# An instruction planner's queue order: X's coordinate rows ahead of Y, a longer plan time for transposing loads, one guard product by a scalar, and the last rows in two stores

## The chip, the cores and the metric

The kernel runs on one core of one Trainium2 chip. The metric is the device time of one execution in microseconds. All inputs and outputs are in HBM; the result is the 2048 x 512 output in bfloat16.

## What is computed

A gated mix of two branches over the same x (2048 x 512): attention with 32 query heads of size 16 that share one key and one value head, and a gMLP with a spatial product over the 2048 rows.

```python
def reference(A_x, A_wq, A_wk, A_wv, A_wo, B_x, B_w_in, B_w_sp, B_b_sp, B_w_out, gate_w):
    x = A_x
    g = _sigmoid((x * gate_w).sum(-1, keepdims=True))
    a = _A_ref(x, A_wq, A_wk, A_wv, A_wo)      # softmax(q k^T / 4) v, 32 heads of 16, one k and one v
    b = _B_ref(x, B_w_in, B_w_sp, B_b_sp, B_w_out)
    return g * a + (1 - g) * b
...
    z = _gelu(jnp.einsum('bsd,df->bsf', x, w_in))
    z1, z2 = z[..., :Fh], _layernorm(z[..., Fh:], axis=-1)      # Fh = 688
    g = jnp.einsum('ts,bsf->btf', w_sp, z2) + b_sp[None, :, None]
    return jnp.einsum('bsf,fd->bsd', z1 * g, w_out)
```

## The kernel before

The kernel does not form the 2048 x 2048 attention weights. It replaces the exponential by a polynomial of third degree, sums the keys and values into moments once, and evaluates for each query a form of degree three in its 16 coordinates. A guard measures the largest query and key norms, and a second, general path (L1128, "slow") runs instead if they are too large; here the first path runs.

Work on the queries is cut into 16 units u = 4 tg + G: tg is a group of 512 rows, G a group of eight heads. For one unit:

- `g_q` (L813) computes the queries Qt on TensorE, ScalarE copies them, and SyncE (SP) writes them to a scratch in HBM, `qe` (L824, four writes).
- `y_load` (L831) reads them back: Y (L833), in two halves of 512 KB, spreads each coordinate over the partitions; X's coordinate rows (L836, two small reads, tag "lin") fill rows 56 to 63 and 120 to 127 of X. X's other rows are squares that ScalarE makes (L850, after TensorE's L846). Both X and Y have two buffers, so unit u takes those of unit u - 2.
- Four times, t and h being 0 or 1, TensorE multiplies X by the moments T3 (L877, four matmuls, "W"); the result fills PSUM banks 0 to 3, always the same ones. VectorE reads the first half of it and multiplies by Y (L888, "Pr"); ScalarE copies the other half to Wt (L892) and GpSimd multiplies it by Y (L893). TensorE then sums over the coordinates (Pr,cs) and adds terms that read X directly (X,M and X,T3d) and Qt (Qt,T2b).
- After the four units of a group, `g_den` (L906) forms the denominators (Rh) and OT (L927), `g_out` (L1011) adds the output products.

In between TensorE does the gMLP: wT (the transposed spatial weights, loaded by transposing DMAs, L975, four for each of four row groups) times z, in groups of 16 steps ahead of which a bias row stands (bspz,ones), evacuated by VectorE (L995, L998), and the output products with wout and wo.

The order is not written by hand. Every operation is added to a list with a priority, a planned duration and what it reads and writes; `Plan.run` (L348) then simulates the five engines with these durations and always takes, of what is ready on the engine that is free first, the lowest priority number. That gives each engine's instruction order; on the chip, engines wait for each other with semaphores. So a number in the plan can move rows on all engines. For DMAs the plan has the time that SP is held and a rate; Y of unit u has priority YPRI + u and YPRI + u + 0.1, the qe writes YPRI + u - 0.1.

The last four output tiles (t2 = 12 to 15) are stored at the very end; SP branches on the guard's flag ahead of the first of them.

Of the kernel before, what the change touches and what calls it, by code (L numbers as in the profile page):

```python
# [10 lines left out]
ALU = mybir.AluOpType  # L11
# [33 lines left out]
DMA_RATE = 230.0  # L45
# [4 lines left out]
YPRI = 2.1  # L50
# [247 lines left out]
class Plan:  # L298
# [8 lines left out]
    def add(self, eng, cost, fn, r=(), w=(), pri=50.0, grp=None, evac=False, dma=0, size=0, chan=None, rate=DMA_RATE, tag="", after=(), opens=(), hold=(), slack=0.0, swp=SWITCH_PRI):  # L307
        t = Task()
        t.alt = eng if isinstance(eng, dict) else {eng: (cost, fn)}
        t.dma, t.bytes, t.chan, t.rate = dma, size, chan, rate  # L310
        t.pri, t.grp, t.tag, t.idx = pri, grp, tag, len(self.tasks)
        t.first = False
        t.users, t.op, t.eng = [], None, None
        t.tiles = getattr(fn, "tiles", WHOLE)
        r, w = list(r), list(w)
        if grp is not None:
            k = ("grp", id(grp))
            if evac:
# [12 lines left out]
        t.opens = [self.lastw[k] for k in opens]
        t.gates = list(hold)
        t.slack = slack
        t.swp = swp
        for d in t.deps:
            d.users.append(t)
        for d in t.opens + t.gates:
            d.users.append(t)
        t.left = len(t.deps) + len(t.opens) + len(t.gates)
        for k in r:  # L340
            self.readers.setdefault(k, []).append(t)
        for k in w:
# [149 lines left out]
def build_kernel(nc, x_d, wq_d, wk_d, wv_d, wo_d, win_d, wsp_d, bsp_d, wout_d, gw_d, out_d):  # L492
    es = ExitStack()
    with es:
        block = es.enter_context(nc.Block())

        def sb(name, shape, dt):
            return es.enter_context(nc.sbuf_tensor(name, shape, dt))

        def dap(t, off, ap):  # L500
            return bass.AP(tensor=t.tensor, offset=off, ap=ap)
# [3 lines left out]
        def bank(b, n=512, off=0):  # L505
            return ps[:, 512 * b + off:512 * b + off + n]
# [7 lines left out]
        qe = nc.dram_tensor("qe", (16 * 16, QP), B16).ap()  # L514
# [33 lines left out]
        X = sb("X", [128, NXU, 4, 512], B16)  # L548
# [6 lines left out]
        outsb = sb("outsb", [128, 4, D], B16)  # L555
# [14 lines left out]
        qk1 = sb("qk1", [128, 8], F32)  # L570
# [25 lines left out]
        out2 = out_d.rearrange("b s d -> (b s) d")  # L596
# [3 lines left out]
        add = pl.add  # L600
# [31 lines left out]
        def load(eng, fn, w, r=(), size=0, n=1, pri=0.0, chan=None, rate=DMA_RATE, tag="", after=(), hold=()):  # L632
            if chan is None:
                chan = "d%d" % nd[0]
                nd[0] += 1
            return add(eng, 3000.0 if rate < DMA_RATE else 560.0 * n, fn, r=r, w=w, dma=16 * n, size=size, pri=pri, chan=chan, rate=rate, tag=tag, after=after, hold=hold)

        def nonc(fn):
            def f(q):
# [11 lines left out]
        def ld_x(c):  # L651
            load("sp", lambda q: q.dma_start(xn[:, 4 * c:4 * c + 4, :], x2[512 * c:512 * c + 512, :].rearrange("(k p) n -> p k n", p=128)), [("xn", c)], size=524288, pri=c, tag="x")
        ld_x(0)
        load("sp", lambda q: q.dma_start(ident[:], id_d), ["id"], size=32768, pri=0)
        for h in range(2):
            load("sp", lambda q, h=h: q.dma_start(win[:, :, FH + 344 * h:FH + 344 * h + 344], win_d[:, FH + 344 * h:FH + 344 * h + 344].rearrange("(dt p) n -> p dt n", p=128)), [("win2", h)], size=352256, pri=0)
# [172 lines left out]
        def y_load(u):  # L829
            o0 = 16 * QP * u  # L830
            yb, ub = u % NY, u % NXU  # L831
            for h in range(2):
                yld[0] = load("sp", lambda q, h=h: q.dma_start(Y[:, yb, 2 * h:2 * h + 2, :, :].rearrange("p j e n -> p (j e n)"), dap(qe, o0 + 2048 * h, [[QP, 16], [0, 8], [1, 2048]])), [("Y", yb, h)], r=[("qe", u)],  # L833
                              size=524288, pri=YPRI + u + 0.1 * h, chan="y%d%d" % (yb, h), tag="Y")

            load("sp", lambda q: [q.dma_start(X[64 * e + 56:64 * e + 64, ub, :, :], dap(qe, o0 + 512 * e, [[QP, 8], [1024, 4], [1, 512]])) for e in range(2)],  # L836
                 [("X", ub, j) for j in range(4)], r=[("qe", u)], size=65536, n=2, pri=YPRI + u + 0.3, chan="lin%d" % ub, tag="lin")

        def squares(u):
            s, ub = u % NQT, u % NXU  # L840
# [18 lines left out]
        def unit(u):  # L859
# [140 lines left out]
        def zl(t2, ft):  # L1000
            if ft < 5:
                return z1[:, ft, 128 * t2:128 * t2 + 128]
            o = 256 * (t2 // 4) + 128 * (t2 % 2)
            return z5[:, o:o + 128]

        def wl(t2, ft):
            return wout[:, ft + (t2 % 4) // 2 if ft == 5 else ft, :]

        tail = []

        def g_out(t2):  # L1011
            tg, i = t2 // 4, t2 % 4
            last = tg == 3
            g = Group("L" if last else "F")
            opens = [] if last else [("z1", ft, tg) for ft in range(6)] + [("OT", tg % 2, 3)]
            for G in range(4):
                add("pe", c_mm(512), mmx(lambda: g.b, 512, 0, OT[:, tg % 2, G, 128 * i:128 * i + 128], wo[:, G, :], G == 0, False), r=["wo", ("OT", tg % 2, G)], grp=g, pri=25, tag="out", opens=opens if G == 0 else [])
            for ft in range(6):
                add("pe", c_mm(512), mmx(lambda: g.b, 512, 0, zl(t2, ft), wl(t2, ft), False, ft == 5), r=["wout", "wout5", "wout6", ("z1", ft, tg)], grp=g, pri=25, tag="out")
            k = t2 % 4  # L1020
            ea = (620.0, lambda a: a.activation(outsb[:, k, :], bank(g.b), ACT.Copy, scale=G1[:, t2:t2 + 1]))  # L1021
            ed = (640.0, lambda v: v.tensor_scalar(outsb[:, k, :], bank(g.b), G1[:, t2:t2 + 1], None, ALU.mult))  # L1022
            add({"act": ea, "dve": ed} if last else {"act": ea}, 0, None, r=["G1"], w=[("ob", k)], grp=g, evac=True, pri=3, tag="fin")
            o = load("sp", lambda q: q.dma_start(out2[128 * t2:128 * t2 + 128, :], outsb[:, k, :]), [("out", t2)], r=[("ob", k)], size=131072, pri=0, chan="o%d" % k, tag="out")
            if last:
                tail.append(o)

# [36 lines left out]
        for tg in range(4):  # L1066
            for G in range(4):
                u = 4 * tg + G
# [29 lines left out]
            return [t.matmul(ps[0:32, 512 * gf.b + 128 * i:512 * gf.b + 128 * i + 128], qkb[:, i, :], ident[:], start=True, stop=True, tile_position=(0, 0)) for i in range(2)]  # L1098
        add("pe", 120.0, fl, r=["qkb", "id"], grp=gf, pri=12, tag="flag")
        add("dve", 350.0, lambda v: v.tensor_reduce(qk1[0:32, 0:2], ps[0:32, 512 * gf.b:512 * gf.b + 256].rearrange("p (i n) -> p i n", i=2), AX.X, ALU.max), w=["qk1"], grp=gf, evac=True, pri=30, tag="guard")  # L1100
        add("dve", 80.0, lambda v: v.tensor_tensor(qk1[0:32, 2:3], qk1[0:32, 0:1], qk1[0:32, 1:2], ALU.mult), r=["qk1"], w=["qk2"], pri=30, tag="guard")  # L1101
        add("dve", 80.0, lambda v: v.tensor_scalar(qk1[0:32, 3:5], qk1[0:32, 0:2], QK_MAX, None, ALU.is_le), r=["qk1"], w=["qk3"], pri=30, tag="guard")
        add("dve", 80.0, lambda v: v.tensor_scalar(qk1[0:32, 5:6], qk1[0:32, 2:3], S_MAX * S_MAX / SLACK, None, ALU.is_le), r=["qk2"], w=["qk4"], pri=30, tag="guard")
        add("dve", 80.0, lambda v: v.tensor_reduce(qk1[0:32, 6:7], qk1[0:32, 3:6], AX.X, ALU.min), r=["qk3", "qk4"], w=["qk5"], pri=30, tag="guard")
# [209 lines left out]
def bass_gated_mix__grouped_kv_mqa__mixer_gmlp__prompt_kernel(  # L1314
    nc, A_x, A_wq, A_wk, A_wv, A_wo, B_x, B_w_in, B_w_sp, B_b_sp, B_w_out, gate_w, out,
):
    build_kernel(nc, A_x, A_wq, A_wk, A_wv, A_wo, B_w_in, B_w_sp, B_b_sp, B_w_out, gate_w, out)
# [29 lines left out]
```

## Time and profile before

| | |
|---|---|
| runs | median 281.47 us, 281.13 to 281.86, three runs |
| profiled execution | 281.9 us, its span 280.1 us |
| granted TensorE clock, mean | 0.997 |
| instructions in the span | 10009 |
| busy shares of TensorE, VectorE, ScalarE, GpSimd | 94%, 62%, 61%, 57% |
| chain that ended last | TensorE 78%, DMA 8%, VectorE 5%, ScalarE 4% |

Times inside the span are counted from its start. In a row of the timeline stand start, duration, engine, line, operation, output and inputs, shapes and how many; in square brackets how long the engine was idle before and what released it. In a row by stretch stand the stretch, its length and each engine's busy time in it (TensorE, its weight loads, VectorE, ScalarE, GpSimd), the granted clock, the share of the DMA engines and GB/s.

### The profile page before, as it was taken

What the parts mean: (1) busy time and instruction counts of PE and PEld (TensorE: products, weight loads), DVE (VectorE), ACT (ScalarE), POOL (GpSimd) and SP (SyncE); (2) the same over time, 40 slices, a digit from 0 to 9 for tenths busy, and PEclk for the clock granted to TensorE, in tenths of its full rate; (3) what the DMA queues carried; (4) which work ended last, traced back from release to release, by engine and by line L of the source; (5) the groups of instructions that cost most, each with busy time, mean ns of one, the idle gap of its engine ahead of it and who ended that gap; (6) DMA issues with size and microseconds to landing.
All of it is one profiled execution on the core that took longest, in us unless ns stands there. A gap on an engine that the chain in (4) does not pass through costs nothing.

```text
span 280.1 us, 10009 instructions
## 1 busy us (share of the span) xinstructions
PE 263.9 (94%) x4356; PEld 121.0 (43%) x4359; DVE 173.3 (62%) x318; ACT 170.8 (61%) x231; POOL 159.2 (57%) x93
## 2 busy tenths in 40 slices
PE   8899999998799999999898999899997999999991
PEld 3587654532243433533343434333442534344560
DVE  2697995474557966554679657635967463695202
ACT  3576888899695656676764856477545468542001
POOL 8693130474938585665857584757657475986000
PEclk9999999999999999999999999999999999999998
DMA  7949937016777988479882615498986335300002
GB/s 195 331 152 273 218 83 148 6 38 169 241 181 101 234 134 197 99 188 224 163 197 61 173 30 159 107 179 125 235 95 164 82 100 154 68 4 4 2 2 80
DMA packets 51019, 37.80 MB, mean 135 GB/s; under 512 B 36021, under 2 KB 46618, under 8 KB 50970
## 3 DMA queue, kind: packets, MB, share of 16 engines
q1 hardware_dynamic: 50970, 37.12, 57.3%
q8 instruction: 35, 0.57, 0.9%
q14 instruction: 14, 0.11, 0.1%
HBM read 24.52 MB, written 4.19 MB: 103 GB/s over the span
## 4 chain that ended last, share of the span: by engine, by line
PE 78%; DMA 8%; DVE 5%; ACT 4%; SPq 2%; issue 1%; DVEq 0%; ACTq 0%
PE ps L608 51%; PE ps L603 12%; PE ps L877 10%; DMA X<-qe 6%; PE ps L956 3%; DVE Pr L888 2%; DMA wT<-in_A_x_dram 2%; PE ps L846 2%; ACT Wt L892 1%; ACT X L850 1%; ACT Q L826 1%; ACT Qt L820 1%; DVE qk L1101 1%; ACT Ns L901 0%; DVE outsb L1022 0%
## 5 line engine op out<-in xcount | busy, mean ns | idle before, releaser
L893 POOL TENSOR_TENSOR Pr<-Wt,Y 128x1024 bf16<-128x1024 bf16 x64 | 136.3, 2130 | 80.1 <-ACT Wt L892 50.0
L888 DVE SCALAR_TENSOR_TENSOR Pr<-ps,T1c,Y 128x1024 bf16<-128x1024 f32 x64 | 82.0, 1282 | 49.4 <-PE ps L877 49.0
L892 ACT ACTIVATE Wt<-ps,T1c 128x1024 bf16<-128x1024 f32 x64 | 71.4, 1116 | 55.7 <-PE ps L877 55.3
L608 PE MATMUL ps<-wT,z 128*32 128x512 bf16 x1280 | 84.8, 380 | 0.0
L608 PEld LDWEIGHTS ps<-wT,z 128*32 128x32 bf16 x1280 | 32.4, 97 | 35.7 <-issue 8.6
L877 PE MATMUL ps<-X,T 64*128 64x512 bf16 x256 | 38.8, 381 | 4.3 <-DVE Pr L888 4.1
L850 ACT ACTIVATE X<-ps 128x1024 bf16<-128x1024 f32 x32 | 31.3, 1022 | 9.8 <-PE ps L846 9.7
L608 PE MATMUL ps<-wout,z 128*32 128x512 bf16 x384 | 26.8, 380 | 0.5 <-DVE z L998 0.5
L995 DVE TENSOR_TENSOR z<-ps,z 128x512 bf16<-128x512 f32 x20 | 13.7, 687 | 13.8 <-PE ps L608 13.6
L603 PE MATMUL ps<-win,xT 128*128 128x344 bf16 x128 | 21.3, 309 | 0.1
L877 PEld LDWEIGHTS ps<-X,T 64*128 64x128 bf16 x256 | 7.3, 94 | 30.0 <-DVE Pr L888 15.7
L608 PE MATMUL ps<-Pr,cs 128*32 128x512 bf16 x256 | 20.0, 381 | 0.0
L937 ACT ACTIVATE z<-ps 128x344 bf16<-128x344 f32 x32 | 14.1, 460 | 7.9 <-PE ps L603 6.2
L608 PE MATMUL ps<-wo,win 128*32 128x512 bf16 x256 | 18.0, 380 | 0.0
L1021 ACT ACTIVATE outsb<-ps,G 128x512 bf16<-128x512 f32 x14 | 9.5, 689 | 13.6 <-PE ps L608 13.6
L902 DVE SCALAR_TENSOR_TENSOR Prd<-ps,T1d,Qt 128x512 bf16<-128x512 f32 x16 | 11.9, 747 | 7.1 <-PE ps L608 6.9
L608 PEld LDWEIGHTS ps<-wout,z 128*32 128x32 bf16 x384 | 9.8, 96 | 11.8 <-issue 2.6
L608 PE MATMUL ps<-xT,wq 128*32 128x512 bf16 x224 | 14.5, 380 | 0.3 <-DVE qm L1049 0.2
L927 DVE SCALAR_TENSOR_TENSOR win<-Ns,S,ps 128x512 bf16<-128x512 f32 x16 | 11.7, 741 | 5.0 <-PE ps L608 5.0
L939 DVE BATCH_NORM_STATS2 bst<-z 128x6 f32<-128x344 bf16 x32 | 14.3, 486 | 0.7 <-ACT z L937 0.7
L967 ACT ACTIVATE z<-ps 128x512 bf16<-128x512 f32 x20 | 11.8, 599 | 4.5 <-PE ps L608 2.6
L603 PEld LDWEIGHTS ps<-win,xT 128*128 128x128 bf16 x128 | 11.5, 97 | 6.0 <-ACT z L937 0.8
(138 smaller groups left out, 285.4 us busy)
## 6 DMA issues: line engine op xcount, KB each, us to landing
Y<-qe SPq DMA_DIRECT2D x32, 512.0 KB, 5.0
wT<-in_A_x_dram SPq DMA_DIRECT2D x4, 512.0 KB, 6.0
qe<-Qt SPq DMA_DIRECT2D x64, 32.0 KB
out_dram<-outsb SPq DMA_DIRECT2D x16, 128.0 KB, 2.8
X<-qe SPq DMA_DIRECT2D x32, 32.0 KB
Pr<-c_third SPq DMA_DIRECT2D x1, 784.0 KB, 9.1
win<-in_B_w_in_dram SPq DMA_DIRECT2D x2, 344.0 KB, 4.7
win<-in_B_w_in_dram SPq DMA_DIRECT2D x1, 688.0 KB, 9.5
```

The source lines that it names most:

```text
L603: return lambda t: t.matmul(bank(b(), n, off), lhsT, rhs, start=start, stop=stop)
L608: return [t.matmul(ps[32 * q:32 * q + 32, 512 * b() + off:512 * b() + off + n], lhsTs[q], rhss[q], start=start, stop=stop, tile_position=( ...
L850: add("act", 1030.0, lambda a, h=h: a.activation(X[:, ub, 2 * h:2 * h + 2, :], bank(g.b + 2 * h, 1024).rearrange("p (j n) -> p j n", j=2), ...
L877: return [p.matmul(bank(gw.b + 2 * i + e), T3[64 * e:64 * e + 64, t, :], X[64 * e:64 * e + 64, ub, 2 * h + i, :], start=True, stop=True, t ...
L888: add("dve", 1290.0, lambda v, wv=wv, pi=pi, yv=yv, t=t: v.scalar_tensor_tensor(Pr[:, pi, :, :], wv(), T1c[:, t:t + 1], yv, ALU.add, ALU.m ...
L892: add("act", 1040.0, lambda a, wv=wv, wi=wi, t=t: a.activation(Wt[:, wi, :, :], wv(), ACT.Identity, bias=T1c[:, t:t + 1]), r=["T1c"], w=[( ...
L893: add("pool", 2130.0, lambda v, wi=wi, pi=pi, yv=yv: v.tensor_tensor(Pr[:, pi, :, :], Wt[:, wi, :, :], yv, ALU.mult), r=[("Y", yb, h), ("W ...
L902: add("dve", 750.0, lambda v: v.scalar_tensor_tensor(Prd[:, u % NPD, :], bank(gd.b), T1d[:, 0:1], Qt[:, s, :], ALU.add, ALU.mult), r=["T1d ...
L937: add("act", 456.0, lambda a, g=g, h=h: a.activation(z2[:, FH * st + 344 * h:FH * st + 344 * h + 344], bank(g.b, 344), ACT.Gelu_apprx_tanh ...
L939: add("dve", 495.0, lambda v, h=h: v.bn_stats(bst[:, st, h, :], z2[:, FH * st + 344 * h:FH * st + 344 * h + 344]), r=[("z2", st, h)], w=[( ...
L967: add("act", 540.0, lambda a: a.activation(z1[:, ft, 512 * tc:512 * tc + 512], bank(g.b), ACT.Gelu_apprx_tanh), w=[("z1", ft, tc)], grp=g, ...
L995: add("dve", 690.0, lambda v: v.tensor_tensor(dst, bank(g.b), dst, ALU.mult), w=[("z1", ft, tc)], grp=g, evac=True, pri=3.5, tag="u")
```

## The change

Four edits, in the functions above. Transposing loads hold SP 4000 instead of 3000 ns in the plan. X's coordinate rows get a priority just under that of their unit's Y instead of behind it. One product of the guard, 32 x 1 elements, is written as tensor by per-partition scalar instead of tensor by tensor. The last four output tiles go out in two stores of two tiles instead of four.

```diff
-            return add(eng, 3000.0 if rate < DMA_RATE else 560.0 * n, fn, ...
+            return add(eng, 4000.0 if rate < DMA_RATE else 560.0 * n, fn, ...
...
             load("sp", lambda q: [q.dma_start(X[64 * e + 56:64 * e + 64, ub, :, :], ...
-                 ... size=65536, n=2, pri=YPRI + u + 0.3, chan="lin%d" % ub, tag="lin")
+                 ... size=65536, n=2, pri=YPRI + u - 0.05, chan="lin%d" % ub, tag="lin")
...
-            o = load("sp", lambda q: q.dma_start(out2[128 * t2:128 * t2 + 128, :], outsb[:, k, :]), ...
-            if last:
-                tail.append(o)
+            if not last:
+                load("sp", lambda q: q.dma_start(out2[128 * t2:128 * t2 + 128, :], outsb[:, k, :]), ...
+            elif k % 2:
+                tail.append(load("sp", lambda q: q.dma_start(out2[128 * t2 - 128:128 * t2 + 128, :].rearrange("(k p) n -> p k n", p=128), outsb[:, k - 1:k + 1, :]), ...
+                                 r=[("ob", k - 1), ("ob", k)], size=262144, pri=0, ...
...
-        add("dve", 80.0, lambda v: v.tensor_tensor(qk1[0:32, 2:3], qk1[0:32, 0:1], qk1[0:32, 1:2], ALU.mult), ...
+        add("dve", 80.0, lambda v: v.tensor_scalar(qk1[0:32, 2:3], qk1[0:32, 0:1], qk1[0:32, 1:2], None, ALU.mult), ...
```

Lines behind the edits move by one or two in the changed kernel (L1101 of the guard becomes L1103, L1024 becomes L1025 or L1027). The orders of the two programs are alike up to the first product of unit 3; from there they differ on all engines. Three places follow.

TensorE, unit 3, from its second product (L877) to its fourth, before:

```order
L877 MATMUL ps<-X,T 128x512 x4
L608 MATMUL ps<-X,M 32x512 x4
L608 MATMUL ps<-Rh,sg 32x128 x16
L608 MATMUL ps<-wT,z 32x512 x8
L608 MATMUL ps<-Qt,T2b 32x512 x4
L608 MATMUL ps<-wT,z 32x512 x20
L877 MATMUL ps<-X,T 128x512 x4
L608 MATMUL ps<-wT,z 32x512 x4
L608 MATMUL ps<-bspz,ones 32x512 x4
L608 MATMUL ps<-wT,z 32x512 x24
L877 MATMUL ps<-X,T 128x512 x4
```

and after:

```order
L877 MATMUL ps<-X,T 128x512 x4
L608 MATMUL ps<-X,M 32x512 x4
L608 MATMUL ps<-Rh,sg 32x128 x16
L608 MATMUL ps<-wT,z 32x512 x24
L877 MATMUL ps<-X,T 128x512 x4
L608 MATMUL ps<-wT,z 32x512 x4
L608 MATMUL ps<-Rh,sg 32x128 x16
L608 MATMUL ps<-wT,z 32x512 x4
L877 MATMUL ps<-X,T 128x512 x4
```

Between the last two products there now stand eight 512-column matmuls and sixteen of 128 columns instead of 32 of 512 columns.

TensorE, unit 6, from its third product to what follows the fourth, before:

```order
L877 MATMUL ps<-X,T 128x512 x4
L608 MATMUL ps<-Q,cs 32x128 x4
L608 MATMUL ps<-wT,z 32x512 x4
L877 MATMUL ps<-X,T 128x512 x4
L608 MATMUL ps<-bspz,ones 32x512 x4
L608 MATMUL ps<-X,T3d 32x512 x4
```

and after:

```order
L877 MATMUL ps<-X,T 128x512 x4
L608 MATMUL ps<-wout,z 32x512 x8
L608 MATMUL ps<-wT,z 32x512 x8
L608 MATMUL ps<-X,T3d 32x512 x4
L877 MATMUL ps<-X,T 128x512 x4
L608 MATMUL ps<-bspz,ones 32x512 x4
```

Two short rows (a norm's sum, Q,cs, and one step of wT) have become 20 matmuls of 512 columns.

SP's queue from the third transposing load of the last row group to X of unit 13, before:

```order
L975 DMA_TRANSPOSE wT<-in_B_w_sp_dram 128x16x128
L1024 DMA out_dram<-outsb 128x512
L833 DMA Y<-qe 128x1x2048 x2
L1024 DMA out_dram<-outsb 128x512
L975 DMA_TRANSPOSE wT<-in_B_w_sp_dram 128x16x128
L836 DMA X<-qe 8x4x512 x2
L824 DMA qe<-Qt 2x16x512 x4
L833 DMA Y<-qe 128x1x2048 x2
L836 DMA X<-qe 8x4x512 x2
```

and after (the two Y ahead of the second transposing load are unit 11's second half and unit 12's first):

```order
L975 DMA_TRANSPOSE wT<-in_B_w_sp_dram 128x16x128
L1025 DMA out_dram<-outsb 128x512
L833 DMA Y<-qe 128x1x2048 x2
L975 DMA_TRANSPOSE wT<-in_B_w_sp_dram 128x16x128
L836 DMA X<-qe 8x4x512 x2
L833 DMA Y<-qe 128x1x2048
L824 DMA qe<-Qt 2x16x512 x8
L833 DMA Y<-qe 128x1x2048 x2
L836 DMA X<-qe 8x4x512 x2
```

The last transposing load and X of unit 12 now stand ahead of unit 12's second half of Y; unit 13's Y and X stand behind eight qe writes instead of four.

More of the change, by code (lines that the diff above doesn't have):

```diff
@@ L635, in load @@
                 nd[0] += 1
-            return add(eng, 3000.0 if rate < DMA_RATE else 560.0 * n, fn, r=r, w=w, dma=16 * n, size=size, pri=pri, chan=chan, rate=rate, tag=tag, after=after, hold=hold)
+            return add(eng, 4000.0 if rate < DMA_RATE else 560.0 * n, fn, r=r, w=w, dma=16 * n, size=size, pri=pri, chan=chan, rate=rate, tag=tag, after=after, hold=hold)
         def nonc(fn):
@@ L836, in y_load @@
             load("sp", lambda q: [q.dma_start(X[64 * e + 56:64 * e + 64, ub, :, :], dap(qe, o0 + 512 * e, [[QP, 8], [1024, 4], [1, 512]])) for e in range(2)],
-                 [("X", ub, j) for j in range(4)], r=[("qe", u)], size=65536, n=2, pri=YPRI + u + 0.3, chan="lin%d" % ub, tag="lin")
+                 [("X", ub, j) for j in range(4)], r=[("qe", u)], size=65536, n=2, pri=YPRI + u - 0.05, chan="lin%d" % ub, tag="lin")
         def squares(u):
@@ L1023, in g_out @@
             add({"act": ea, "dve": ed} if last else {"act": ea}, 0, None, r=["G1"], w=[("ob", k)], grp=g, evac=True, pri=3, tag="fin")
-            o = load("sp", lambda q: q.dma_start(out2[128 * t2:128 * t2 + 128, :], outsb[:, k, :]), [("out", t2)], r=[("ob", k)], size=131072, pri=0, chan="o%d" % k, tag="out")
-            if last:
-                tail.append(o)
+            if not last:
+                load("sp", lambda q: q.dma_start(out2[128 * t2:128 * t2 + 128, :], outsb[:, k, :]), [("out", t2)], r=[("ob", k)], size=131072, pri=0, chan="o%d" % k, tag="out")
+            elif k % 2:
+                tail.append(load("sp", lambda q: q.dma_start(out2[128 * t2 - 128:128 * t2 + 128, :].rearrange("(k p) n -> p k n", p=128), outsb[:, k - 1:k + 1, :]), [("out", t2)],
+                                 r=[("ob", k - 1), ("ob", k)], size=262144, pri=0, chan="o%d" % k, tag="out"))
         gw4 = Group("any")
@@ L1100, in build_kernel @@
         add("dve", 350.0, lambda v: v.tensor_reduce(qk1[0:32, 0:2], ps[0:32, 512 * gf.b:512 * gf.b + 256].rearrange("p (i n) -> p i n", i=2), AX.X, ALU.max), w=["qk1"], grp=gf, evac=True, pri=30, tag="guard")
-        add("dve", 80.0, lambda v: v.tensor_tensor(qk1[0:32, 2:3], qk1[0:32, 0:1], qk1[0:32, 1:2], ALU.mult), r=["qk1"], w=["qk2"], pri=30, tag="guard")
+        add("dve", 80.0, lambda v: v.tensor_scalar(qk1[0:32, 2:3], qk1[0:32, 0:1], qk1[0:32, 1:2], None, ALU.mult), r=["qk1"], w=["qk2"], pri=30, tag="guard")
         add("dve", 80.0, lambda v: v.tensor_scalar(qk1[0:32, 3:5], qk1[0:32, 0:2], QK_MAX, None, ALU.is_le), r=["qk1"], w=["qk3"], pri=30, tag="guard")
```

## The prediction

> **What bounds the kernel now.** I read the page's busy shares first, then the busy time by stretch, then the timeline at the stretches where TensorE idles.
>
> ```profile
> PE 263.9 (94%) x4356; PEld 121.0 (43%) x4359; DVE 173.3 (62%) x318; ACT 170.8 (61%) x231; POOL 159.2 (57%) x93
> ```
>
> ```profile
> 0.00:90.00 90.00, 84.58 (x1150) 44.58 (x1152) 59.33 (x175) 67.53 (x114) 46.65 (x41) 1.00 0.66 165
> 90.00:135.00 45.00, 45.00 (x800) 18.99 (x796) 27.98 (x35) 29.79 (x37) 29.05 (x14) 1.00 0.80 175
> 135.00:152.00 17.00, 14.69 (x268) 5.61 (x260) 13.68 (x20) 10.52 (x12) 11.94 (x7) 1.00 0.74 159
> 152.00:170.00 18.00, 18.00 (x310) 7.41 (x308) 10.76 (x15) 11.89 (x14) 11.95 (x6) 1.00 0.39 106
> 170.00:178.00 8.00, 6.75 (x137) 3.50 (x135) 6.85 (x11) 3.87 (x4) 4.48 (x3) 1.00 0.29 82
> 178.00:208.00 30.00, 30.00 (x524) 12.08 (x520) 19.12 (x24) 18.50 (x21) 21.09 (x10) 1.00 0.95 169
> 208.00:219.00 11.00, 9.48 (x160) 3.49 (x148) 6.60 (x7) 4.50 (x5) 6.38 (x3) 1.00 0.46 113
> 219.00:255.00 36.00, 36.00 (x648) 15.27 (x648) 23.14 (x27) 21.26 (x23) 25.43 (x12) 1.00 0.30 79
> 255.00:280.00 25.00, 19.43 (x396) 10.02 (x392) 5.85 (x8) 2.98 (x4) 2.25 (x2) 0.97 0.08 25
> ```
>
> First number after the stretch is its length, second TensorE's busy time. TensorE is the bound. The programs hold the same 4359 matmuls and change tile shape equally often (165 times), so the changed order can only remove or add TensorE idle time. Both orders are the same on TensorE until about 94 us; the 5.4 us idle in the first 90 us stay. Behind that there are three idle pieces: 17.00 - 14.69 = 2.31 us, 8.00 - 6.75 = 1.25 us and 11.00 - 9.48 = 1.52 us, and the tail.
>
> **The three pieces.** A "product" below is the four matmuls of L877; they use one PSUM area, so the next product waits until VectorE (L888) and ScalarE (L892) have read the last one.
>
> ```profile
> 136.40 0.61 PE L877 MATMUL ps<-X,T 64*128 64x512 bf16 x4
> 137.12 1.28 DVE L888 SCALAR_TENSOR_TENSOR Pr<-ps,T1c,Y 128x1024 bf16<-128x1024 f32 x1 [1.28 <-PE ps L877]
> 138.46 0.60 PE L877 MATMUL ps<-X,T 64*128 64x512 bf16 x4 [1.07 <-DVE Pr L888]
> 148.13 0.24 PE L608 MATMUL ps<-Q,cs 128*32 128x128 bf16 x4 [0.19 <-DVE z L995]
> 149.32 0.60 PE L877 MATMUL ps<-X,T 64*128 64x512 bf16 x4 [0.95 <-DVE Pr L888]
> ```
>
> ```profile
> 134.42 2.06 PE ps L608 x36
> 152.19 1.84 PE ps L608 x32
> ```
>
> Start to start no two products can stand closer than 138.46 - 136.40 = 2.06 us. Four more 512-column matmuls (one "quad") cost 2.06 - 1.84 = 0.22 us. A product takes 0.54 us on the chain, so with eight quads between two of them they stand 0.54 + 1.84 = 2.38 us apart, and with n quads 2.38 - 0.22 (8 - n). Below n = 6.5 TensorE idles 2.06 minus that. Sixteen 128-column matmuls count as one quad. In the old order two pairs have n = 1.25 (Q,cs x4 and wT x4; Rh x16 and Q,cs x4): 0.90 us, so 1.16 idle each, where the rows show 1.07 and 0.95 + 0.19.
>
> The second piece is the guard on VectorE:
>
> ```profile
> 171.99 2.13 POOL L893 TENSOR_TENSOR Pr<-Wt,Y 128x1024 bf16<-128x1024 bf16 x1 [3.82 <-ACT Wt L892]
> 172.45 1.68 DVE L1101 TENSOR_TENSOR qk<-qk 32x1 f32<-32x1 f32 x1
> 172.58 0.60 PE L877 MATMUL ps<-X,T 64*128 64x512 bf16 x4
> 174.47 2.12 POOL L893 TENSOR_TENSOR Pr<-Wt,Y 128x1024 bf16<-128x1024 bf16 x1 [0.36 <-PE ps L956]
> 174.51 0.14 DVE L1105 TENSOR_SCALAR flag<-qk 32x1 int32<-32x1 f32 x1
> 174.59 1.28 DVE L888 SCALAR_TENSOR_TENSOR Pr<-ps,T1c,Y 128x1024 bf16<-128x1024 f32 x1
> 175.93 0.61 PE L877 MATMUL ps<-X,T 64*128 64x512 bf16 x4 [1.00 <-DVE Pr L888]
> ```
>
> One product of 32 numbers takes 1.68 us and ends when GpSimd's instruction ends (171.99 + 2.13 = 174.12). The product of 172.58 could have been read at 172.58 + 0.72 = 173.30 and is read at 174.59.
>
> The third is X's coordinate rows (L836), which queue behind both halves of Y:
>
> ```profile
> 198.22 6.33 SPq L975 DMA_TRANSPOSE wT<-in_B_w_sp_dram  x1
> 208.98 1.27 SPq L833 DMA_DIRECT2D Y<-qe  x2
> 210.29 0.82 SPq L836 DMA_DIRECT2D X<-qe  x2
> ```
>
> ```profile
> 216.93 0.40 PE L608 MATMUL ps<-X,T3d 128*32 128x512 bf16 x4 [1.52 <-DMA X<-qe]
> ```
>
> **The change, part by part**, against the profiled execution's 281.9 us (span 280.1; the median of the runs is 281.47, 0.4 lower).
>
> - The asking order and the longer plan time of the transposes add no instruction; together they re-sort all queues from about 94 us on. Between unit 7's second and third product now stand nine quads, between unit 6's last two five (wout x8, wT x8, X,T3d x4), so both old waits go. Gain 2.31 us. New sparse pairs: unit 3's last (wT x4, Rh x16, wT x4: n = 3, so 2.06 - 1.28 = 0.78), unit 6's last (n = 5, so 2.06 - 1.72 = 0.34) and unit 8's first (Rh x16, wT x4, X,M x4, wT x8: n = 5, 0.34). Cost 1.46 us. All other pairs behind 94 us have seven quads or more in both orders.
> - Guard's product by a scalar: 1.68 becomes about 0.14 (the row of L1105, the same engine with one SBUF tensor, under a running GpSimd instruction). The guard then ends 1.5 us earlier, at 173.1 on the old clock, before the 173.30 at which L888 is wanted. Gain 1.25; none, if it still waits for GpSimd.
>  [...] The row of L1105, 0.14 us in the shadow of a 2.12 us GpSimd instruction, speaks against it here.
> - X of unit 13: the transposing load in front of it now stands one half of Y earlier, so Y's halves are no longer issued back to back in 1.27 us but as GpSimd frees them, and X meets less ahead of it. Gain 1.52; zero if it lands as before (6.07 us after issue).
> - X elsewhere. X of units 5, 6, 9 and 10 is issued behind Y's second half and four qe writes, and now used sooner.
>
> ```profile
> L893 POOL TENSOR_TENSOR Pr<-Wt,Y 128x1024 bf16<-128x1024 bf16 x64 | 136.3, 2130 | 80.1 <-ACT Wt L892 50.0
> L892 ACT ACTIVATE Wt<-ps,T1c 128x1024 bf16<-128x1024 f32 x64 | 71.4, 1116 | 55.7 <-PE ps L877 55.3
> ```
>
> ```profile
> 156.25 2.50 SPq L824 DMA_DIRECT2D qe<-Qt  x4
> 158.79 0.81 SPq L836 DMA_DIRECT2D X<-qe  x2
> ```
>
> ```profile
> 163.44 0.39 PE L608 MATMUL ps<-X,T3d 128*32 128x512 bf16 x4
> ```
>
> ```profile
> 81.31 5.29 DMA X<-qe
> 210.81 6.07 DMA X<-qe
> ```
>
>  For unit 9: Y's last half is free after a product's 0.7 + 1.12 (L892) + 2.13 (L893) = 4.0 us, then 0.6 for Y, 2.5 for qe, 0.5 to X's second issue: 7.6 us. TensorE has four products and 37 quads and one squares pass up to the use: 37 x 0.22 + 4 x 0.62 + 0.5 = 11.1 us. That leaves 3.5 us; units 5, 6 and 10 come to 3.5 to 3.9 in the same way. Old unit 9, in the same queue order, was used 163.44 - 159.2 = 4.2 us after its second issue (half of 0.81 us behind 158.79) with no idle time; the late ones took 5.29 and 6.07. So 0 to 2.5 us each; nearest is old unit 9, and I take 0.5 for all four.
> - VectorE's evacuations of PSUM banks (L927, L995) now stand in other places between two L888, and four TensorE rows (T2b of unit 4, the bias rows ahead of three wT groups in units 8, 14 and 15) come up just when VectorE has two or three of them queued. Such waits are short before:
>
> ```profile
> PEld ps L608 <- DVE qm L1049: 2.6, 7, 0.5
> ```
>
>  Seven waits came to 2.6 us with 0.5 the longest, so 0 to 2.0 us for four; I take 0.3 each, 1.2.
> - Last rows in two stores:
>
> ```profile
> 274.58 1.41 DVE L1022 TENSOR_SCALAR outsb<-ps,G 128x512 bf16<-128x512 f32 x2 [0.72 <-PE ps L608]
> 275.36 2.79 SPq L1024 DMA_DIRECT2D out_dram<-outsb  x4
> ```
>
> ```profile
> Y<-qe SPq DMA_DIRECT2D x32, 512.0 KB, 5.0
> out_dram<-outsb SPq DMA_DIRECT2D x16, 128.0 KB, 2.8
> ```
>
>  The second store waits for VectorE's last row at 274.58 + 1.41 = 275.99. Landing lies between 2.8 us (128 KB) and 5.0 (512 KB); for 256 KB a line through both gives 3.5, so 279.5, where the last store landed shortly before the span's end of 280.1. The two issues saved (2.79 us for four) were in the shadow of the landings. I take zero, from -0.7 to +0.5.
>
> Sum: -2.31 + 1.46 - 1.25 - 1.52 + 0.5 + 1.2 + 0 = -1.9 us: 280.0 for the profiled execution, 279.5 at the median.
>
> **Rivals**, at the median's level.
> 1. X late in units 5, 6, 9, 10 (slower). If all four land like unit 3's 5.29 us, each is 1.4 to 1.8 us short, 6 in sum, where 0.5 is counted: 285. It turns the sign where the four waits exceed 2.4 us, that is at a landing of 4.3 us. For it: the two rows of 5.29 and 6.07. Against: old unit 9.
> 2. Unit 13's X is late again, behind Y as before: 281.0. For it: X still stands behind both halves of Y in the queue, and four more qe writes (2.50 us of SP) stand ahead of those. Against: the 6.33 us transposing load stands farther ahead, so SP reaches Y before GpSimd has freed it.
> 3. The guard's product still waits for GpSimd: 280.8.
> 4. The short waits and X cost nothing: 279.5 - 1.7 = 277.8.
>
> **How the numbers follow.** Forecast 279.5 (278.4 to 280.6): 0.60. Rival 1: 0.08; rival 2: 0.14; rival 3: 0.06; rival 4: 0.12. A measurement of this kernel tells about 0.3% from no change, 0.84 us. Faster holds the forecast and rival 4 and a little of 2 and 3: 0.74; the rest of these is the same: 0.18; slower is rival 1: 0.08. The range from 277.8 to 281.3 leaves out rival 1 and the edges.
>
> **What the profile after would show.** TensorE full from 135 to 152 us but for 0.3 at unit 6's last pair; a new idle piece of about 0.8 us near 100 us, released by L888; L1103 at about 0.15 us and no idle piece behind it; no wait on X near 217 us. Waits on X near 112, 126, 165 or 178 us would be rival 1. I would be wrong if VectorE, out of step behind unit 3, held up more products than the three counted, or if the landings of X depend on the transposing loads issued right behind them.

## The result, and the profile after

The changed kernel takes 277.61 us (median of four runs, 276.77 to 278.24) where the kernel before, beside it, took 281.50: a ratio of 0.986, interval 0.983 to 0.989, 3.9 us less. The forecast was 279.5 us, in a range from 277.8 to 281.3. The sign was right, the gain about twice the forecast, and the median lies 0.2 us below the range. The profiled execution is the fastest of the four: 276.8 us, span 275.0.

The page of the changed kernel has TensorE at 96% of a shorter span, with nearly the same busy time (264.5 us; 263.9 before, where three matmuls have no record):

```profile
PE 264.5 (96%) x4359; PEld 121.8 (44%) x4359; DVE 171.1 (62%) x318; ACT 170.8 (62%) x231; POOL 159.2 (58%) x93
```

Its busy time by the stretches that the prediction used (stretch, length, TensorE's busy time, then its weight loads, VectorE, ScalarE, GpSimd; clock, DMA share, GB/s):

```profile
0.00:90.00 90.00, 86.36 (x1176) 46.04 (x1180) 60.60 (x177) 68.93 (x116) 48.01 (x41) 1.00 0.68 167
90.00:135.00 45.00, 44.38 (x796) 18.45 (x784) 27.47 (x34) 29.31 (x35) 28.34 (x15) 1.00 0.77 172
135.00:152.00 17.00, 16.74 (x312) 6.94 (x308) 13.72 (x20) 9.96 (x12) 11.93 (x6) 1.00 0.80 156
152.00:170.00 18.00, 17.49 (x327) 7.90 (x319) 10.87 (x16) 11.59 (x14) 11.29 (x6) 1.00 0.39 105
170.00:178.00 8.00, 8.00 (x120) 2.87 (x120) 5.28 (x11) 4.54 (x6) 5.53 (x3) 1.00 0.71 168
208.00:219.00 11.00, 11.00 (x220) 5.08 (x215) 7.55 (x9) 5.20 (x7) 8.06 (x4) 1.00 0.30 65
```

The three old pieces of idle time (2.31, 1.25 and 1.52 us) are gone; the 17.00 - 16.74 = 0.26 us between 135 and 152 us are a new wait, at 137.35 below. What TensorE waits for behind 94 us (engine and line, what it waited for, us in total, how often, the longest), before and then after:

```profile
PE ps L877 <- DVE Pr L888: 3.0, 3, 1.1
PE ps L608 <- DMA X<-qe: 1.5, 1, 1.5
PE ps L608 <- issue: 0.3, 1, 0.3
PE ps L608 <- DVE z L995: 0.2, 1, 0.2
```

```profile
PE ps L877 <- DVE Pr L888: 1.1, 3, 0.6
PE ps L608 <- DVE z L998: 0.5, 1, 0.5
PE ps L608 <- DVE z L995: 0.3, 1, 0.3
PE ps L608 <- DVE win L927: 0.2, 1, 0.2
```

(The wait on L998, 0.53 us, is in both, at 273.9 us before, just outside that window.) The 0.3 us under "issue" in the list of before is no wait. A bias matmul of 512 columns (bspz,ones) stands there: the trace has its weight load, at 170.84, and lacks the record of the matmul itself. The row ahead of it and the row behind it start 171.16 - 170.63 = 0.53 us apart; in the trace of after, which has the record (at 169.26), they start 169.58 - 169.06 = 0.52 us apart. So of the second piece's 1.25 us only 1.00 was a wait.

The new waits, in the timeline:

```profile
96.52 0.61 PE L877 MATMUL ps<-X,T 64*128 64x512 bf16 x4
98.50 0.61 PE L877 MATMUL ps<-X,T 64*128 64x512 bf16 x4 [0.62 <-DVE Pr L888]
137.35 0.61 PE L877 MATMUL ps<-X,T 64*128 64x512 bf16 x4 [0.26 <-DVE Pr L888]
158.96 0.60 PE L877 MATMUL ps<-X,T 64*128 64x512 bf16 x4 [0.25 <-DVE Pr L888]
160.21 0.40 PE L608 MATMUL ps<-bspz,ones 128*32 128x512 bf16 x4 [0.26 <-DVE z L995]
249.80 0.40 PE L608 MATMUL ps<-bspz,ones 128*32 128x512 bf16 x4 [0.25 <-DVE win L927]
```

The first row is unit 3's third product. The three waits on L888 are the short pairs of units 3, 6 and 8 that the prediction named; the last two are bank waits, two of the four counted.

To compare executions I cut each trace in three: up to unit 3's first product (TensorE's order is the same there in every kernel), from there to the end of the last matmul, and from there to the span's end.

| trace | front, us | middle, us | idle in the middle | tail, us |
|---|---|---|---|---|
| before | 93.09 | 181.87 | 5.62 | 5.13 |
| after | 91.74 | 178.52 | 2.17 | 4.70 |
| guard_alone | 92.82 | 181.79 | 5.33 | 5.01 |
| guard_single | 92.99 | 180.66 | 4.28 | 5.41 |
| after_tensor_guard | 92.19 | 178.52 | 2.42 | 4.68 |
| x_ahead_alone | 92.37 | 180.46 | 3.33 | 5.13 |
| transposes_4000_alone | 91.78 | 180.90 | 4.37 | 5.15 |
| t5000_x_behind | 92.18 | 177.36 | 1.39 | 3.99 |
| after_pairs_made | 91.67 | 180.72 | 4.43 | 4.67 |
| before_x13_first | 91.47 | 181.80 | 5.34 | 5.08 |
| stores_alone | 91.96 | 182.28 | 5.82 | 4.68 |
| after_x_before_qe | 93.12 | 178.52 | 2.42 | 4.98 |
| t5000_x_2_3_first | 92.49 | 177.32 | 1.37 | 3.84 |

In eight of these traces (all but after, x_ahead_alone, transposes_4000_alone and the two of t5000) the idle time holds the 0.25 us of the matmul without a record.

The front varies by 1.65 us: with the landing of the first loads (the first product of all starts at 48.43 us before and at 47.95 after) and with that of X of units 2 and 3, for which TensorE waits 1.37 us before and 0.50 after. SP's queue is the same in both up to there, so 1.35 of the 5.1 us between the spans 280.1 and 275.0 is chance and no effect of the change. The middle repeats where the order does: all three traces with the changed kernel's TensorE order have 178.52. The four with the old order and the old wait behind the guard have 181.79 to 182.28; they differ by a stop that the part on the third piece tells of. So the change is worth 181.87 - 178.52 = 3.35 us in the middle and 0.4 in the tail, 3.8 in sum, near the 3.9 of the medians.

### The profile page after: what moved, and what is told of

Read it like the earlier page. It is cut to its first block, busy times and chain, and to the rows that moved or that the text cites. A ratio compares the mean times of both kernels' runs of the same rounds, so it can differ in the third digit from the quotient of the medians.

```text
span 275.0 us, 10010 instructions
## 1 busy us (share of the span) xinstructions
PE 264.5 (96%) x4359; PEld 121.8 (44%) x4359; DVE 171.1 (62%) x318; ACT 170.8 (62%) x231; POOL 159.2 (58%) x93
## 4 chain that ended last, share of the span: by engine, by line
PE 83%; DMA 5%; ACT 4%; DVE 3%; issue 2%; SPq 1%; DVEq 0%; ACTq 0%
PE ps L608 54%; PE ps L603 13%; PE ps L877 11%; DMA X<-qe 4%; PE ps L956 3%; PE ps L846 2%; DMA gwl<-in_gate_w_dram 1%; DVE Pr L888 1%; ACT Wt L892 1%; ACT X L850 1%; DVE win L927 1%; ACT Qt L820 1%; ACT Q L826 1%; DVE outsb L1022 0%; PE ps L773 0%
## 5 line engine op out<-in xcount | busy, mean ns | idle before, releaser
L888 DVE SCALAR_TENSOR_TENSOR Pr<-ps,T1c,Y 128x1024 bf16<-128x1024 f32 x64 | 82.0, 1281 | 59.5 <-PE ps L877 59.2
L877 PE MATMUL ps<-X,T 64*128 64x512 bf16 x256 | 38.8, 381 | 2.4 <-DVE Pr L888 2.2
L877 PEld LDWEIGHTS ps<-X,T 64*128 64x128 bf16 x256 | 7.4, 94 | 28.8 <-DVE Pr L888 17.3
L901 ACT ACTIVATE Ns<-ps 128x512 f32<-128x512 f32 x16 | 9.6, 598 | 10.7 <-PE ps L608 8.9
```

The costliest lines, as they stand in the source:

```text
L877: return [p.matmul(bank(gw.b + 2 * i + e), T3[64 * e:64 * e + 64, t, :], X[64 * e:64 * e + 64, ub, 2 * h + i, :], start=True, stop=True, t ...
L888: add("dve", 1290.0, lambda v, wv=wv, pi=pi, yv=yv, t=t: v.scalar_tensor_tensor(Pr[:, pi, :, :], wv(), T1c[:, t:t + 1], yv, ALU.add, ALU.m ...
```

## The experiments

Each kernel was timed beside the kernel before, whose median was 281.1 us in these runs; ratios are to it, with a 95% interval (a ratio on record is not exactly that of the two medians).

**The guard.** The prediction gave the guard's wait to the form of L1101. First that edit alone:

```diff
-... v.tensor_tensor(qk1[0:32, 2:3], qk1[0:32, 0:1], qk1[0:32, 1:2], ALU.mult), ...
+... v.tensor_scalar(qk1[0:32, 2:3], qk1[0:32, 0:1], qk1[0:32, 1:2], None, ALU.mult), ...
```

> The kernel before with the guard's product by a scalar and nothing else; all queues keep their order, so the product L1101 stands where GpSimd runs L893. Theory form (the prediction's): the scalar form does not wait for GpSimd, L1101 falls from 1.68 to about 0.15 us and TensorE's 1.00 us of waiting for L888 behind it goes, with the 0.25 us ahead of it: 1.0 to 1.25 us less, 280.2 to 280.5. Theory place: the scalar form still waits for GpSimd's instruction to end, L1101 stays at 1.3 to 1.7 us, 281.4, and the changed kernel got rid of the wait only because its order puts the guard where GpSimd stands idle.

Measured: 281.24 us, ratio 1.0015 (0.9986 to 1.0043). Nothing is gained, as the place theory has it, and yet L1101 no longer waits, as the form theory has it. The guard in its timeline:

```profile
171.72 2.13 POOL L893 TENSOR_TENSOR Pr<-Wt,Y 128x1024 bf16<-128x1024 bf16 x1 [3.82 <-ACT Wt L892]
172.18 0.20 DVE L1101 TENSOR_SCALAR qk<-qk 32x1 f32<-32x1 f32 x1
172.31 1.55 DVE L1102 TENSOR_SCALAR qk<-qk 32x2 f32<-32x2 f32 x1
174.22 1.28 DVE L888 SCALAR_TENSOR_TENSOR Pr<-ps,T1c,Y 128x1024 bf16<-128x1024 f32 x1
175.56 0.61 PE L877 MATMUL ps<-X,T 64*128 64x512 bf16 x4 [0.89 <-DVE Pr L888]
```

L1101 does run under GpSimd's instruction, in 0.20 us. The next row, L1102, with two numbers a partition, now takes 1.55 us and ends at 173.86, where GpSimd's ends (171.72 + 2.13 = 173.85). The wait moved by one instruction. So I wrote L1102 as two rows of one number:

```diff
-... v.tensor_scalar(qk1[0:32, 3:5], qk1[0:32, 0:2], QK_MAX, None, ALU.is_le), ...
+... [v.tensor_scalar(qk1[0:32, 3 + i:4 + i], qk1[0:32, i:i + 1], QK_MAX, None, ALU.is_le) for i in range(2)], ...
```

> The kernel with the guard's product by a scalar alone, and its next guard operation (L1102, which compares two numbers a partition, 32x2) written as two operations of one number each; all queues keep their order. In the run with the scalar form alone the wait moved: L1101 took 0.20 us, but L1102 then took 1.55 and ended where GpSimd's instruction ended. Theory two elements (an operation whose row has two or more elements, or two SBUF tensors, waits for GpSimd; one with one element and one tensor does not): all guard rows take 0.14 to 0.20 us, L888 comes at once, 1.0 to 1.15 us less than with the scalar alone, a ratio of 0.996 to before. Rival: whichever guard operation comes second waits for GpSimd; the wait stays, ratio 1.000.

Measured: 280.66 us, ratio 0.9986 (0.996 to 1.0012); by time alone no difference can be told. The trace tells it:

```profile
171.88 2.13 POOL L893 TENSOR_TENSOR Pr<-Wt,Y 128x1024 bf16<-128x1024 bf16 x1 [3.83 <-ACT Wt L892]
172.35 0.20 DVE L1101 TENSOR_SCALAR qk<-qk 32x1 f32<-32x1 f32 x1
172.48 0.19 DVE L1102 TENSOR_SCALAR qk<-qk 32x1 f32<-32x1 f32 x2
173.19 1.28 DVE L888 SCALAR_TENSOR_TENSOR Pr<-ps,T1c,Y 128x1024 bf16<-128x1024 f32 x1
174.76 0.61 PE L877 MATMUL ps<-X,T 64*128 64x512 bf16 x4
```

All guard rows pass under GpSimd's instruction, L888 follows, and the product behind it waits no more: idle time between 170 and 180 us is 0.25 (the matmul without a record) where it was 1.14 with the scalar alone, 0.9 us less. So of the guard's TENSOR_SCALAR rows, which read one SBUF tensor, those of one element did not wait for GpSimd (0.13 to 0.20 us each under its instruction), and the row of two elements did (1.55 us). (L1104, a TENSOR_REDUCE that reads three numbers and writes one, took 0.14 us under the same instruction.) Why the second element makes the difference, no run shows.

In the changed kernel the product L1103 as tensor by tensor again:

```diff
-... v.tensor_scalar(qk1[0:32, 2:3], qk1[0:32, 0:1], qk1[0:32, 1:2], None, ALU.mult), ...
+... v.tensor_tensor(qk1[0:32, 2:3], qk1[0:32, 0:1], qk1[0:32, 1:2], ALU.mult), ...
```

> The changed kernel with the guard's product back as tensor by tensor; all queues keep their order. Theory place (in the new order the guard stands where GpSimd is idle): L1103 takes about 0.2 us, no wait of TensorE behind it, and the time is the changed kernel's, a ratio of 0.986 to before. Theory form (the scalar form is what saved 1.25 us): 1.0 to 1.25 us more, 0.990 to 0.9905.

Measured: 277.20 us, ratio 0.9854 (0.9817 to 0.9892); middle 178.52, as with the scalar form. The scalar form is worth nothing there; the product of two tensors takes no longer:

```profile
170.51 0.15 DVE L1103 TENSOR_TENSOR qk<-qk 32x1 f32<-32x1 f32 x1
```

In the changed kernel the guard's rows stand ahead of a unit's first product, in a pause of GpSimd:

```profile
166.05 2.13 POOL L893 TENSOR_TENSOR Pr<-Wt,Y 128x1024 bf16<-128x1024 bf16 x1 [0.25 <-ACT Wt L892]
170.06 0.20 DVE L1103 TENSOR_SCALAR qk<-qk 32x1 f32<-32x1 f32 x1
170.19 0.15 DVE L1104 TENSOR_SCALAR qk<-qk 32x2 f32<-32x2 f32 x1
170.85 1.28 DVE L888 SCALAR_TENSOR_TENSOR Pr<-ps,T1c,Y 128x1024 bf16<-128x1024 f32 x1
172.02 2.13 POOL L893 TENSOR_TENSOR Pr<-Wt,Y 128x1024 bf16<-128x1024 bf16 x1 [3.84 <-PE ps L608]
```

Between 168.18 and 172.02 GpSimd does nothing, and even the row of two elements takes 0.15 us. In the changed kernel it was the guard's place, not the form, that took the wait away.

**Which edit moves the order to the better.** X's priority alone, and the transposes' plan time alone, in the kernel before:

```diff
-... pri=YPRI + u + 0.3, chan="lin%d" ...
+... pri=YPRI + u - 0.05, chan="lin%d" ...
```

> The kernel before with X asked ahead of Y in the plan and nothing else (transposes at 3000 ns). Theory order (only where TensorE's rows come to stand matters): this plan has short pairs of products only in unit 11 (third to last, 3 quads: X,T3d x4 and Rh x32) and unit 15 (second to third, 5 quads); by the after trace's 0.62 and 0.25 us that is 0.87 us in place of 2.31; the guard stands ahead of its product there as in the changed kernel (1.25 less), the last transposing load stands ahead of unit 12's second half of Y (1.52 less), and bank waits cost 0.5 to 1.0: 277.8 to 278.4. Rival X early (what gains is X's rows landing earlier, the longer plan time adds nothing): as the changed kernel without its stores and scalar, 278.0, with no wait on X behind 95 us. Rival both needed: the gain comes only with the longer transposes, 280 or more.

```diff
-... 3000.0 if rate < DMA_RATE ...
+... 4000.0 if rate < DMA_RATE ...
```

> The kernel before with transposing loads counted as 4000 ns and nothing else (X behind Y as before). Theory order: four short pairs behind 94 us (unit 3 last 3 quads; unit 7 first to second 3.25; unit 8 second to third 4.25; unit 11 second to third 3): 0.62 + 0.58 + 0.38 + 0.62 = 2.2 us, as much as the 2.31 before; unit 13's X is no longer late (the last transposing load stands ahead of unit 12's second half of Y): 1.5 less; the guard's wait between 0 and 1.25 less; bank waits 0.5 to 1.0 more: 279.6 to 280.8. Rival X early: without X's new priority nothing is gained, 281.5. Rival transposes (they carry the gain): 278.

Measured: X alone 279.87 us, ratio 0.9957 (0.9939 to 0.9975), middle 1.4 us shorter; transposes alone 280.30, 0.9976 (0.996 to 0.9992), 1.0 shorter. Neither carries the gain alone, and the two do not add up: 1.4 + 1.0 is 2.4, both together 3.35. The first missed its expected 277.8 to 278.4: TensorE's longest waits behind 94 us show most of why.

```profile
PE ps L608 <- DVE qm L1049: 0.9, 1, 0.9
PE ps L877 <- DVE Pr L888: 0.8, 2, 0.6
PE ps L608 <- DVE z L998: 0.5, 1, 0.5
PE ps L608 <- DVE z L995: 0.3, 1, 0.3
PE ps L608 <- DVE win L927: 0.3, 1, 0.3
PE ps L608 <- DVE Rh L921: 0.2, 1, 0.2
```

The two short pairs cost 0.8 us, as counted (0.87); the bank waits 0.9 + 0.3 + 0.3 + 0.2 = 1.7, more than the 0.5 to 1.0 allowed. The waits are not all: TensorE's busy time in the middle is 180.46 - 3.33 = 177.13 us, where before, with the matmul without a record counted in, it is 181.87 - 5.62 + 0.25 = 176.50. These 0.6 us are not explained; part of them may be short waits, since a 512-column matmul's record lasts 0.38 us while 32 of them take 1.84 us, so that, by my estimate from these two, a wait of under 0.3 us would leave no idle time. With the transposes alone the four pairs came as counted (2.4 us against 2.2); its longest waits:

```profile
PE ps L877 <- DVE Pr L888: 2.4, 4, 0.7
PE ps L846 <- DVE Pr L888: 0.7, 1, 0.7
PE ps L608 <- DVE win L927: 0.5, 2, 0.3
```

If the order is all that counts, a better order with X asked as late as before should do better than the changed kernel:

```diff
-... 3000.0 if rate < DMA_RATE ...
+... 5000.0 if rate < DMA_RATE ...
```

with the changed kernel's guard and stores, and X at YPRI + u + 0.3:

> The kernel before with transposing loads counted 5000 ns, X asked behind Y as before, and with the changed kernel's guard and stores. Theory order (what counts is where products and bank users come to stand on TensorE): behind 94 us this plan has one short pair only (unit 11's last, Rh x32 and Pr,cs x8, 4 quads: about 0.45 us) where the changed kernel has 0.62 + 0.26 + 0.25; bank waits 0.3 to 0.8 where it has 0.5; the guard stands just ahead of a product in a stretch of wo and wout rows; 0.2 to 0.9 us less than the changed kernel, a ratio of 0.983 to 0.985 to before. Rival X early (X's priority carries the gain): X behind Y is late again in units 5 to 13, 0.992 or more.

Measured: 275.26 us, ratio 0.9788 (0.9753 to 0.9823), the fastest kernel of this study, 2 us below the changed one. Of its waits behind 94 us these are left:

```profile
PE ps L608 <- DVE win L927: 1.0, 2, 0.7
PE ps L877 <- DVE Pr L888: 0.4, 1, 0.4
```

X is never waited for there (behind 94 us it lands 0.66 us or more ahead of use). So the gain does not need X ahead of Y, and where X was moved up and nothing else (three runs below), nothing was gained. Against the changed kernel the middle is 178.52 - 177.36 = 1.16 us shorter, somewhat more than the expected 0.2 to 0.9, and the tail 4.70 - 3.99 = 0.7 us, which was not expected: the last tiles come out one by one and ScalarE alone evacuates them.

**What a short pair costs.** In the changed kernel three products are moved later so that three quads instead of eight follow each:

```diff
+pe = pg.ops["pe"]
+prods = [o for o in pe if o.tag == "W"]
+for k, n in [(37, 5), (42, 5), (46, 5)]:
+    i = pe.index(prods[k])
+    pe.insert(i + n, pe.pop(i))
```

> The changed kernel with three products moved five rows of four matmuls later on TensorE (unit 9's second, unit 10's third, unit 11's third), so that each has three quads behind it up to the next product instead of eight; nothing else moves. Theory pair (a product that comes too soon leaves TensorE idle, and no later work makes it good): three idle pieces released by L888, each 0.62 us as unit 3's in the after trace, 1.9 us more, a ratio of 0.992 to before; by the prediction's formula 0.78 each, 2.3 us, 0.994. Rival absorbed (VectorE's lateness is made good by the quads that now stand ahead of the moved product): 0 to 0.3 us more, 0.986.

Measured: 279.03 us, ratio 0.9945 (0.9916 to 0.9974), middle 2.2 us longer. The wait on L888 behind 94 us rises from 1.1 to 3.1 us, three more of 0.69, 0.69 and 0.62:

```profile
PE ps L877 <- DVE Pr L888: 3.1, 6, 0.7
```

```profile
174.23 1.28 DVE L888 SCALAR_TENSOR_TENSOR Pr<-ps,T1c,Y 128x1024 bf16<-128x1024 f32 x1 [2.17 <-PE ps L877]
175.57 0.61 PE L877 MATMUL ps<-X,T 64*128 64x512 bf16 x4 [0.69 <-DVE Pr L888]
```

Nothing makes it good later. A pair with three quads costs 0.62 to 0.69 us, below the formula's 0.78. The other 0.2 us of the middle do not show as idle time and are not explained.

**The third piece.** X of unit 13 asked ahead of its Y in the kernel before:

```diff
+sp = pg.ops["sp"]
+x13 = [o for o in sp if o.tag == "lin"][13]
+sp.remove(x13)
+sp.insert(sp.index([o for o in sp if o.tag == "Y"][26]), x13)
```

> The kernel before with X of unit 13 asked ahead of both halves of its Y on SP (about 1.4 us earlier); nothing else moves. Four traces with this order show 1.2 to 1.7 us of TensorE idle between 205 and 217 us: once as a wait on X of unit 13 (the kernel before), three times as a stop near 207 us that no semaphore ends, in a run of wT rows, with X on time. Theory X: the idle time is X's; it goes, 1.2 to 1.5 us less, 0.995 to before. Theory crowd (the last transposing load, 5 to 6 us long, holds up whatever is asked for behind it, X or TensorE's own instructions): the stop near 207 us stays and nothing is gained in most executions, 0.998 to 1.000.

Measured: 281.16 us, ratio 1.0000 (0.9973 to 1.0027). X of unit 13 now landed at 211.29, 3.7 us ahead of its use (a weight load at 215.03), and TensorE stood still all the same, inside a run of wT rows:

```profile
203.66 1.03 PE L608 MATMUL ps<-wT,z 128*32 128x512 bf16 x13
205.93 0.40 PE L608 MATMUL ps<-wT,z 128*32 128x512 bf16 x3 [1.25 <-issue]
```

The traces of guard_alone, stores_alone and guard_single, which have the same TensorE order, stop at the same instruction, for 1.34, 1.73 and 1.18 us, and have no wait on X there; only the first trace of the kernel before had the wait on X instead. In these three and in before_x13_first the records of the DMA queues show one 16 KB block on an instruction queue that ends 1.25 to 1.34 us ahead of TensorE's next matmul, and that begins 1.9 to 2.2 us after SP has let go of the last transposing load; in the trace of before the block began at 202.83, inside that load's hold, ended at 203.92 and came in time. The changed kernel's profile page has 35 such blocks (queue q8, 0.57 MB), and 4359 matmuls and 4359 weight loads of TensorE among 10010 instructions; that the blocks are mostly TensorE's is my estimate from these numbers, the trace does not tell whose they are. If they are, the last transposing load (4.9 to 6.3 us on SP) seems to have held up either X or TensorE's code. In the changed kernel it is issued at 191.85 instead of 198.22, and neither is late. That the load is the cause is not shown: no run moves it by itself.

**The stores.** Two stores for the last four tiles, alone (the diff as in the change):

> The kernel before with the last four rows in two stores and nothing else; all queues keep their order up to the stores. The prediction took 0 (from -0.7 to +0.5). From the two traces: the end of the last matmul to the span's end was 280.1 - 274.96 = 5.1 us before and 275.0 - 270.26 = 4.7 us after. Theory tail: 0.4 us less, 281.1, since two issues less stand between VectorE's last row and the last landing. Rival: the tail's 0.4 us is chance, 281.5 and a tail of 5.1 us again.

Measured: 280.77 us, ratio 1.0000 (0.9973 to 1.0026): the runs cannot tell 0.4 us. The tails can: with four stores 5.13, 5.01, 5.41, 5.13, 5.15 and 5.08 us, with two, on the same last rows, 4.70, 4.68, 4.68, 4.67 and 4.98. The means are 5.15 and 4.74, 0.4 us apart. In the changed kernel:

```profile
269.88 1.41 DVE L1022 TENSOR_SCALAR outsb<-ps,G 128x512 bf16<-128x512 f32 x2 [0.72 <-PE ps L608]
270.73 1.68 SPq L1027 DMA_DIRECT2D out_dram<-outsb  x2
```

VectorE's last row ends at 271.29, the second store is issued at 271.37, landed at 274.49, 3.1 us later (counted: 3.5). Before, the last of four was issued at 277.72, 1.7 us behind VectorE's last row, and landed at 279.54. The issues were not in the shadow of the landings: the last one starts late.

**X's margin.** In the changed kernel X of four units ahead of the qe writes that stand in front of it:

```diff
+lin = [o for o in sp if o.tag == "lin"]
+for u in (5, 6, 9, 10):
+    i = sp.index(lin[u])
+    j = i
+    while sp[j - 1].tag == "qw":
+        j -= 1
+    sp.insert(j, sp.pop(i))
```

> The changed kernel with X of units 5, 6, 9 and 10 asked ahead of the four qe writes that stand in front of it on SP (2.5 us earlier); the other queues keep their order. In the after trace these four landed 0.11, 0.39, 0.35 and 0.34 us ahead of their use. Theory thin margin (in executions where a landing takes longer TensorE waits): 0 to 0.8 us less than the changed kernel, a ratio of 0.983 to 0.986 to before, and the four land 2 us or more ahead of use. Rival: the margin always held, 0.986. Rival collision: X earlier meets Y in the queue, lands later and delays Y, 0.987 or more.

Measured: 277.26 us, ratio 0.9854 (0.9816 to 0.9891), middle 178.52 as without it. The four land 1.66 to 2.71 us ahead of use. The thin margin had cost nothing.

The same for units 2 and 3 in the fastest kernel, where every trace has a wait on X:

> The kernel with transposing loads at 5000 ns and X behind Y, with X of units 2 and 3 asked ahead of the four qe writes in front of them on SP (2.5 us earlier); nothing else moves. In its trace TensorE waits up to 0.2 us for X of unit 2 and 0.55 for X of unit 3, in the others 0.3 to 1.1 and 0.15 to 0.55. Theory late X: both waits go, 0.5 to 1.0 us less, a ratio of 0.975 to 0.977 to before. Rival collision: X asked right behind 1 MB of Y lands no sooner (it landed 4.7 and 5.2 us after issue), 0.979.

Measured: 275.43 us, ratio 0.9798 (0.9771 to 0.9826), nothing gained. X of unit 2 landed at 70.49 instead of 73.17 and its wait, under 0.2 us, went; X of unit 3, asked 2.6 us earlier (77.92), landed at 86.00, 8.1 us after issue, where it had landed at 85.68, and TensorE's one wait on X grew from 0.6 to 1.2:

```profile
PE ps L608 <- DMA X<-qe: 1.2, 1, 1.2
```

Why it landed no sooner is open.

## Why the prediction was right in sign and wrong in size

| term | forecast | measured |
|---|---|---|
| old short pairs (units 6, 7) go | -2.31 | -2.31 |
| new short pairs (units 3, 6, 8) | +1.46 | 0.62 + 0.26 + 0.25 = +1.13 |
| guard's wait | -1.25 | -1.00 |
| unit 13's X | -1.52 | -1.52 |
| X of units 5, 6, 9, 10 | +0.5 | 0 |
| bank waits | +1.2 | 0.26 + 0.25 = +0.51 |
| last rows in two stores | 0 | -0.4 |
| sum of the terms | -1.9 | -3.6 |
| middle and tail of the two traces | | -3.8 |

The last 0.2 us stand in none of these terms.

**The main mechanism held.** TensorE was the bound (94% busy before, 96% after), its busy work stayed (263.9 us, without three matmuls, and 264.5), and the idle pieces came and went with the pairs of products, at the places named. after_pairs_made shows the cost of a pair by making three.

**The step that failed is the size of what the new order costs.** The sum set 1.46 + 0.5 + 1.2 = 3.16 us of new waits against the gains; the trace has 1.13 + 0 + 0.51 = 1.64. With the stores, taken as hidden, four terms err by 1.9 us to the same side. Bank waits: 0.3 each for four, where two came at 0.26 and 0.25, 0.7 us too much. X: 0.5 where the four landed in 3.46, 3.66, 3.51 and 3.61 us after their second issue and were used 0.11, 0.39, 0.35 and 0.34 us later. The issue-to-use time was worked out well (3.6 to 4.1 against 3.5 to 3.9 forecast), and no cost followed, since landing stayed like old unit 9's (3.60 us). Pairs: the formula took 2.06 us from product to product, while unit 3's last two stand 98.50 - 96.52 = 1.98 apart, and the three cost 0.1 to 0.2 less each. Stores: taken as hidden, worth 0.4. A fifth term errs the other way: the guard's 1.25 us were read off a stretch's busy time, which lacks the 0.25 us of the matmul without a record; the prediction's own row has the wait, 1.00.

**The range** stopped at rival 4's own value, with X and the bank waits free, and did not add the lower end that the prediction itself gives the stores, -0.7. With it the range would have begun at 277.1.

**Two gains came by luck, for another reason than the one given.** The guard's wait went because the new order put the guard into a pause of GpSimd; the form of L1101 alone gave nothing, since L1102 behind it waited in its place (1.55 us). Rival 3 named the row, L1101, that did not wait (0.20 us). The prediction went by L1105, a row of one element (0.14 us), and did not ask which row of the guard has two. And the third piece did not hang on X's place behind Y: in four of five traces of the old order it is a stop with X on time, and with X first the stop stayed. What the prediction said of the transposing load's place is what is left, as far as the traces go; it is argued, not shown.

**The signs named beforehand** came true: 0.3 us at unit 6's last pair, a new idle piece near 100 us (0.62, at 98.5, released by L888), L1103 at 0.20 without an idle piece, no wait on X near 217. Rival 1's waits, near 112, 126, 165 or 178 us, did not come, though the margin was 0.1 to 0.4 us.

## What to carry to other kernels

Where a planner sets the order, an edit of one number is worth what the new order makes of the bound engine's waits, not what the number says: the two plan edits were worth 1.4 and 1.0 us alone, 3.35 together, and another plan time for the transposing loads, without X's new priority, did better than both. Cut the traces into a part that varies by chance and a part that repeats (here 178.52 us three times), and compare the latter: the interval of the runs was 0.8 us to each side. A part that repeats in one order need not in another (181.79 to 182.28 in the old one). Before idle time is called a wait, see whether a matmul's record is missing there (0.25 us here). And when a sum has several unknown costs, let the range go to the sum of their lower ends, not to the end of one.

## What the runs showed of the hardware that was not expected

- VectorE's TENSOR_SCALAR on 32x2 numbers of SBUF took 1.55 us under a GpSimd instruction and 0.15 in its pause; on 32x1 it took 0.13 to 0.20 under such an instruction.
- TensorE stopped 1.18 to 1.73 us inside a run of matmuls in four of five traces of one order, with no semaphore in the trace that ended it, and went on 1.25 to 1.34 us after a 16 KB block of an instruction queue had come.
- X's small reads (two of 32 KB) landed from 1.9 to 8.4 us after the second issue; asked 2.6 us earlier, one landed 0.3 us later.
